# Shift rows in front of the sums, and query products in cycles of 18 score tiles

## The chip, the cores and the metric

The kernel runs on one core of a Trainium2 chip. The metric is the device time of one launch in microseconds (us), the median of several runs. Of the core's engines, TensorE (PE; its weight loads are listed apart as PEld) does the matrix products, ScalarE (ACT) the exponentials, VectorE (DVE) copies, reductions and splits, GpSimd (POOL) squares and some preparation, and SyncE (SP) issues the transfers.

## The reference

Two layers of attention and two of a token mixer, in turn, with the same weights both times. x is 2048 x 512, float32.

```python
x = x + A(layernorm(x)); x = x + B(layernorm(x))      # and both once more

def A(x):                                  # 32 heads of 16, one shared key and value head
    q = heads(x @ wq); k = x @ wk; v = x @ wv
    p = softmax(q k^T / 4)
    return concat(p v) @ wo

def B(x):                                  # over the tokens, F = 1792
    u = gelu(layernorm(x)^T @ w1 + b1)
    return (u @ w2 + b2)^T
```

## The kernel before

**Attention in score tiles.** The queries of a layer are 32 groups: 4 blocks of 512 queries, each with 8 groups of 4 heads. A group takes 32 score tiles, one for each of 16 key tiles and each of two pairs of heads, so a layer has 1024. A score tile is two matmuls into one of three double banks of PSUM (`scores`, L952), 51 rows deep: the queries and keys are split in a rounded part and a rest, and three rows more carry the shift. ScalarE takes exp into SBUF (L962). Every few tiles VectorE first copies the tile out of PSUM (L960) so that the bank comes free early, and ScalarE then works in SBUF; a "copied" tile below is such a one. Then come the sums (L968): two matmuls that multiply the exps by the values and a column of ones, each into its own strip of 32 columns of the group's bank. [...] Sums lag behind scores by two tiles at the end of a cycle. When a group's last sum is done, VectorE copies its bank out (L870), and divisions and the output product follow as side work.

**Cycles.** What order PE works in is written out in `Attention.run` by tuples. A number k > 0 means k tiles' scores, 13 a trio whose last tile is copied, -4 the sums of the four oldest tiles, 0 a piece of other work. The rest of an attention layer's query products are such pieces up to tile 256 or so, each of two halves of 6 matmuls (`in_halves`, L462 for the matmuls):

- WHOLE, 12 tiles: `(13, 0, 0, 13, -4, 13, -4, 13, -4)`, both halves behind the first trio.
- LONG, 16 tiles: `(2, 0, 13, -4, 13, -4, 13, 0, 13, -4, 12, -4)`, the halves apart.
- TINY, 4 tiles: `(2, 0, 2, -4)`, the piece being the shift rows of a block.
- PLAIN, 2 tiles, with no piece.

`Proj.later` (L688) lists the pieces in order; `run` takes the head of that list, turns WHOLE into LONG where there is slack, and takes PLAIN where a cycle would reach over a guard (a branch at tiles 64 and 256 of layer 0, 128 and 256 of layer 1, behind which the kernel picks the way by a bound of the scores). In the first drain behind a product's second half, `put_queries` rounds the queries (VectorE, L554 and L569), squares them (GpSimd, L565) and stores them to DRAM (SP, L574). From there `load_group` brings a group's queries (L831) and shift rows (L824) to one of two buffers.

**Shift rows.** For each block, `shifts` (L584 to L596) multiplies the squared queries by `sel`, a table that sums a head's 16 rows. Its four matmuls (L590), one for each 128 rows of queries, add into the same 32 rows of a PSUM bank, a row for each head. VectorE takes their minimum over the block (L594) and copies them (L595), and SP stores them (`put_shifts`, L757). The minima go by DRAM to one row (`store_lowest` L641, `load_lowest` L646), from which the guard's flag is worked out.

**The bank of a piece.** Pieces use the bank that the next group's sums will use (`spare`), so a piece must be read out before that group's first sums. Behind tile 256 pieces are the mixer's products, in other cycles.

Of the kernel before, what the change touches and what calls it, by code (L numbers as in the profile page):

```python
# [38 lines left out]
WHOLE = (13, 0, 0, 13, -4, 13, -4, 13, -4)  # L39
LONG = (2, 0, 13, -4, 13, -4, 13, 0, 13, -4, 12, -4)  # L40
# [11 lines left out]
TINY = (2, 0, 2, -4)  # L52
# [37 lines left out]
def kernel(  # L90
# [40 lines left out]
    sel = cp.tile([P, ND, H], BF16, tag="sel", name="sel")  # L131
# [3 lines left out]
    qmin = cp.tile([H, NB + 1], F32, tag="qmin", name="qmin")  # L135
# [5 lines left out]
    fd = dp.tile([3, H, NB], F32, tag="fd", name="fd")  # L141
# [18 lines left out]
    def constants():  # L160
# [19 lines left out]
        for m in range(ND):  # L180

            nc.gpsimd.affine_select(
                sel[:, m, :], sel[:, m, :], pattern=[[-DH, H]], compare_op=ALU.is_ge,
                fill=0.0, base=P * m, channel_multiplier=1,
            )
            nc.gpsimd.affine_select(
                sel[:, m, :], sel[:, m, :], pattern=[[DH, H]], compare_op=ALU.is_ge,
                fill=0.0, base=DH - 1 - P * m, channel_multiplier=-1,
            )
# [84 lines left out]
    class Proj:  # L274
# [11 lines left out]
        def open(self):  # L286
# [6 lines left out]
            self.c2 = k.tile([H, 2, QB], F32R, tag="c2", name=f"c2_{n}")  # L293
# [44 lines left out]
        def empty(self, eng=None):  # L338
            eng = eng or nc.vector
            if self.l == 0:  # L340
                nc.vector.memset(f32(self.wkv), 0.0)
            eng.memset(f32(self.c2), 0.0)
            self.ones = self.pool.tile([P, P], F32, tag="ones", name=f"ones{self.l}")
            eng.memset(self.ones, -SHIFT)
# [241 lines left out]
        def shifts(self, b, pc=None, parts=range(ND)):  # L586

            pc = (bank2(f"pc{self.l}_{b}")[:, 0, :] if pc is None else pc)[:H, :]
            for m in parts:
                nc.tensor.matmul(  # L590
                    pc, sel[:, m, :], self.sq.pop((b, m)), start=(m == parts[0]), stop=(m == parts[-1])
                )
            c = b + 1 if b or parts[0] else 0
            nc.vector.tensor_reduce(qmin[:, c : c + 1], pc, axis=AX.X, op=ALU.min)  # L594
            nc.vector.tensor_copy(self.c2[:, 0, :], pc)  # L595
            put_shifts(self.c2, NG * b + 2 * parts[0], NG * b + 2 * parts[-1] + 2, 8 * parts[0])  # L596
# [46 lines left out]
        def load_lowest(self, j, k):  # L643

            self.far = sm.tile([1, H, NB - 1], F32, tag="far", bufs=1, name=f"far{self.l}_{j}")
            nc.sync.dma_start(self.far[:, :, :k], fd[j : j + 1, :, :k])  # L646
# [40 lines left out]
        def later(self, att):  # L687

            n, work = self.l, []
# [7 lines left out]
            def rows(b, parts=range(ND)):  # L697
                put(TINY, [lambda i: self.shifts(b, bank(i, f"pc{n}_{b}"), parts)])

            def far(j, lo, hi):  # L700
                then(-1, lambda: self.lowest(j, lo, hi))
# [5 lines left out]
            if n == 0:  # L707
                project(0, range(2, ND))
                then(-1, lambda: (self.first.release(), att.weights()))
                rows(0, range(1, ND))  # L710
# [18 lines left out]
            for j in range(2 - n):  # L729
                k = j + (3 if n == 0 else 2)  # L730
                then(k, lambda j=j: att.split_weights(j))
            far(2, 2, NB + 1)
            return work
# [100 lines left out]
    class Attention:  # L834
        def __init__(self, layer):
# [5 lines left out]
            self.behind, self.lag, self.pieces = None, LAG, []  # L841
# [181 lines left out]
        def slack(self, later):  # L1023

            left = 2 * NKT * NG - self.scored - sum(self.size(t) for t, _, _ in later)
            return left - (48 if self.scored < 2 * NKT * 5 else 12)

        def run(self, mix, proj):
# [10 lines left out]
            while self.scored < total:  # L1039
                mix.chores(self)  # L1040
                ahead = min(t for t in guards if t > self.scored)
                known = ahead < guards[-2] or not later
# [3 lines left out]
                if turn is None:  # L1046
                    turn = PLAIN
                    self.lag = 2 * LAG if mix.normed and self.scored < total - 16 else LAG
                    if len(self.pend) == self.lag:
                        after, queued = None, bool(later) and not mix.projections  # L1050
                        if queued:
                            turn, parts, after = later[0]
                            if turn is WHOLE and self.to_boundary() >= 14 and self.slack(later) >= 4:
# [6 lines left out]
                    if queued and turn is LONG and left < self.size(LONG):  # L1060
# [7 lines left out]
                    if turn is WHOLE and self.to_boundary() == 2:  # L1068
                        turn = PLAIN
                parts = list(parts)  # L1070
                for k in turn:
                    if k > 0:
                        self.more(mix, k)
                    elif k == 0:
                        if queued and turn is TINY:
# [828 lines left out]
```

## Time and profile before

| | |
|---|---|
| time, median of 3 runs | 2494.57 us (2494.18 to 2497.32) |
| the profiled execution | 2495.04 us, span 2493.2, granted clock 0.998 |
| tiles 12 to 244, layer 0 | 232.60 us (57.67 to 290.27) |
| tiles 12 to 244, layer 1 | 227.13 us (1302.06 to 1529.19) |
| scores on PE, L952 | 684.8 us, sums L968 1000.4 us |
| exps on ACT, L962 | 1406.5 us from PSUM, 655.8 us from copied tiles |
| query products L462 | 81.0 us in 312 matmuls of the common form |
| shift rows: L590, L594, L595 | 8.3, 6.1 and 6.0 us |

Times in the table are busy times of groups but for the first four rows. A row of the timeline gives a start, a length, the engine, the line, what is written from what, and how many instructions it holds; in brackets stands how long the engine was idle before, and what ended that. A PE row's length runs to the end of its last matmul, which reaches into the next row; differences of starts are the better measure of what a row costs. A row of the waits gives a sum, a count and the longest.

### The profile page before, as it was taken

How to read it: one execution, taken by the hardware profiler on the slowest of the kernel's cores; microseconds unless marked ns; L12 is line 12 of the kernel's file. 1: busy time of each engine (PE TensorE's matmuls, PEld its weight loads, DVE VectorE, ACT ScalarE, POOL GpSimd, SP SyncE). 2: the span in 40 equal slices, each digit the busy share in tenths (PEclk: the TensorE clock that was granted, in tenths of full speed). 3: DMA queues.
4: the chain of work that ended last, by engine and by line, in shares of the span. 5: the costliest groups of instructions: out<-in, count | busy, mean ns of one | idle time of the engine just before them, and what ended most of it. 6: DMA issues, size and time to landing. Idle time of an engine off the chain costs nothing. (4 is left out here: it accounts for less than half of the span.)

```text
span 2493.2 us, 43495 instructions
## 1 busy us (share of the span) xinstructions
PE 2476.1 (99%) x16704; PEld 1253.2 (50%) x16704; DVE 1693.1 (68%) x2691; ACT 2148.4 (86%) x2430; POOL 160.6 (6%) x288
## 2 busy tenths in 40 slices
PE   9999999999999999999999999999999999999999
PEld 6444344444444444489964443444444444445898
DVE  6565566667766776579954664666677667765797
ACT  6999999999999999754459999999999999996643
POOL 5000000000000000140320000000000000002300
PEclk9999999999999999999999999999999999999999
DMA  3231201111111111153253211111111111111543
GB/s 126 75 98 44 66 27 39 34 39 31 39 32 41 31 40 31 33 152 89 60 184 118 59 48 49 31 39 31 40 31 40 32 41 31 40 31 44 143 119 94
DMA packets 168528, 147.80 MB, mean 59 GB/s; under 512 B 16723, under 2 KB 132977, under 8 KB 167537
## 3 DMA queue, kind: packets, MB, share of 16 engines
q1 hardware_dynamic: 168304, 144.85, 19.6%
q8 instruction: 137, 2.24, 0.4%
q14 instruction: 87, 0.70, 0.1%
HBM read 99.17 MB, written 28.84 MB: 51 GB/s over the span
## 5 line engine op out<-in xcount | busy, mean ns | idle before, releaser
L962 ACT ACTIVATE p<-sc 128x1024 f32<-128x1024 f32 x1444 | 1406.5, 1049 | 64.2 <-PE sc L952 63.1
L960 DVE COPY p<-sc 128x1024 f32<-128x1024 f32 x604 | 739.2, 1224 | 522.6 <-PE sc L952 437.8
L968 PE MATMUL acc<-p,vaug 128*32 128x512 f32 x8192 | 1000.4, 600 | 0.0
L952 PE MATMUL sc<-qs,kst 51*128 51x512 f32 x4096 | 684.8, 432 | 7.2 <-SPq L668 3.4
L962 ACT ACTIVATE p<-p 128x1024 f32<-128x1024 f32 x604 | 655.8, 1086 | 13.6 <-DVE p L960 8.8
L952 PEld LDWEIGHTS sc<-qs,kst 51*128 51x128 f32 x4096 | 338.3, 185 | 561.5 <-ACT p L962 387.8
L968 PEld LDWEIGHTS acc<-p,vaug 128*32 128x32 f32 x8192 | 218.9, 109 | 488.9 <-issue 473.6
L1247 PE MATMUL pu<-hb,w 128*128 128x512 f32 x792 | 209.7, 406 | 0.0
L1234 POOL TENSOR_TENSOR w<-w1r,w 128x256 fp32r<-128x256 f32 x86 | 68.5, 806 | 1583.3 <-ACT w L1232 1583.1
L1247 PEld LDWEIGHTS pu<-hb,w 128*128 128x128 f32 x792 | 140.9, 188 | 57.7 <-issue 31.8
L1476 ACT CAST w<-rA 128x896 fp32r<-128x896 f32 x88 | 82.8, 944 | 95.8 <-PE pyX L1598 46.1
L888 DVE RECIPROCAL o<-o 128x128 f32<-128x128 f32 x120 | 113.3, 944 | 8.9 <-DMA o<-ev 8.9
L1477 DVE TENSOR_TENSOR w<-rA,w 128x896 fp32r<-128x896 f32 x88 | 95.5, 1087 | 14.4 <-ACT w L1476 13.5
L929 PE MATMUL po<-wo,hl 128*128 128x512 f32 x360 | 100.7, 413 | 0.1
L1598 PE MATMUL pyY<-u,w 128*128 128x256 f32 (+1 forms) x392 | 88.7, 328 | 0.0
L870 DVE COPY ev<-acc 128x512 f32<-128x512 f32 x64 | 43.7, 683 | 62.8 <-PE acc L968 62.8
L462 PE MATMUL pq<-hT,wq 128*128 128x512 f32 x312 | 81.0, 403 | 0.0
L929 PEld LDWEIGHTS po<-wo,hl 128*128 128x128 f32 x360 | 62.6, 188 | 34.0 <-issue 16.0
L1247 PE MATMUL pu_l<-hb,w 128*128 128x512 f32 x336 | 77.1, 389 | 0.0
L1232 ACT CAST w<-w1r 128x256 fp32r<-128x256 f32 x86 | 34.1, 406 | 49.4 <-PE pu_l L1247 14.1
L1598 PEld LDWEIGHTS pyY<-u,w 128*128 128x128 f32 x392 | 68.4, 189 | 6.5
L1598 PE MATMUL pyX<-u,w 128*128 128x256 f32 (+1 forms) x420 | 70.9, 325 | 0.0
(232 smaller groups left out, 1795.4 us busy)
## 6 DMA issues: line engine op xcount, KB each, us to landing
w1r<-in_B_w_dram SPq DMA_DIRECT2D x224, 128.0 KB
rA<-in_B_w_dram SPq DMA_DIRECT2D x64, 448.0 KB
qs<-qd SPq DMA_DIRECT2D x384, 64.0 KB
qd<-q SPq DMA_DIRECT2D x64, 256.0 KB
o<-ev SPq DMA_DIRECT2D x128, 128.0 KB
x<-in_A_x_dram SPq DMA_DIRECT2D x16, 256.0 KB
hd<-hT SPq DMA_DIRECT2D x2, 2048.0 KB
out_dram<-x SPq DMA_DIRECT2D x10, 256.0 KB
```

What stands on the lines that cost most here:

```text
L462: yield nc.tensor.matmul(out, a, c, start=(k == 0), stop=(k == len(terms) - 1))
L888: nc.vector.reciprocal(o[:, 1, c], o[:, 1, c])
L929: nc.tensor.matmul(po, a, c, start=(k == 0), stop=(k == 3 * len(parts) - 1))
L952: nc.tensor.matmul(sc[:, j, :], kst[kt // 4][rows, kt % 4 * P : (kt % 4 + 1) * P], qs[i % NQ][rows, j0 // 2, :], start=True, stop=True,)
L960: nc.vector.tensor_copy(pt, sc)
L962: nc.scalar.activation(pt, sc, AF.Exp, scale=0.25)
L968: nc.tensor.matmul(self.acc[i][c : c + 32, :], vaug[:, kt].rearrange("p d k -> p (d k)"), pt[:, j, :], start=(kt == 0), stop=(kt == NKT - ...
L1234: eng.tensor_tensor(w[:, 1], raw, f32(w[:, 0]), op=ALU.subtract)
L1247: nc.tensor.matmul(pu, a, c, start=(start and k == 0), stop=(stop and k == 5))
L1476: nc.scalar.copy(out[:, 0], src)
L1477: nc.vector.tensor_tensor(out[:, 1], src, f32(out[:, 0]), op=ALU.subtract)
L1598: nc.tensor.matmul(out, a, c, start=start and k == i == 0 and len(terms) == 3, stop=(k == NFH - 1 and i == len(terms) - 1), skip_group_che ...
```

## The change

A new cycle BROAD of 18 tiles holds both halves behind its first trio, as WHOLE does, and then five trios more. `run` takes it for a query product with a slack of 6 tiles or more, in layer 0 only if no shift rows hang on the product; otherwise LONG or WHOLE as before. TINY is gone. The shift rows become a `tail` of the product in front of them, run in front of the sums of a later drain of the same cycle (the third behind the product), or of the PLAIN cycle that follows; until then no other piece is begun. The four matmuls of the rows now each write their own 32 rows of the bank, so that `sel` is one table instead of four, `qmin` and the copy cover 128 rows, and the rows of a block go out in four transfers of 8 rows instead of one of 32. The two calls of `split_weights` and the bound's load move by one entry with it.

```diff
+BROAD = (13, 0, 0, 13, -4, 13, -4, 13, -4, 13, -4, 13, -2)
-TINY = (2, 0, 2, -4)
...
-        def shifts(self, b, pc=None, parts=range(ND)):
-            pc = (bank2(f"pc{self.l}_{b}")[:, 0, :] if pc is None else pc)[:H, :]
+        def shifts(self, b, pc=None, parts=range(ND), new=0):
+            pc = bank2(f"pc{self.l}_{b}")[:, 0, :] if pc is None else pc
             for m in parts:
                 nc.tensor.matmul(
-                    pc, sel[:, m, :], self.sq.pop((b, m)), start=(m == parts[0]), stop=(m == parts[-1])
+                    pc[H * m : H * m + H, :], sel, self.sq.pop((b, m)), start=True, stop=True,
+                    skip_group_check=True,
                 )
...
-            nc.vector.tensor_reduce(qmin[:, c : c + 1], pc, axis=AX.X, op=ALU.min)
-            nc.vector.tensor_copy(self.c2[:, 0, :], pc)
-            put_shifts(self.c2, NG * b + 2 * parts[0], NG * b + 2 * parts[-1] + 2, 8 * parts[0])
+            nc.vector.tensor_reduce(qmin[rows, c : c + 1], pc[rows, :], axis=AX.X, op=ALU.min)
+            nc.vector.tensor_copy(self.c2[rows, 0, :], pc[rows, :])
+            for m in parts[new:]:
+                put_shifts(self.c2, NG * b + 2 * m, NG * b + 2 * m + 2, H * m)
...
-            def rows(b, parts=range(ND)):
-                put(TINY, [lambda i: self.shifts(b, bank(i, f"pc{n}_{b}"), parts)])
+            def rows(b, parts=range(ND), new=0):
+                tails[len(work) - 1] = [lambda i: self.shifts(b, bank(i, f"pc{n}_{b}"), parts, new)]
...
-                        after, queued = None, bool(later) and not mix.projections
-                        if queued:
-                            turn, parts, after = later[0]
-                            if turn is WHOLE and self.to_boundary() >= 14 and self.slack(later) >= 4:
+                        after, queued = None, bool(later) and not mix.projections and not self.tail
+                        if self.tail:
+                            turn, parts = PLAIN, []
+                        elif queued:
+                            turn, parts, after, tail = later[0]
+                            room = self.slack(later) if turn is WHOLE and (self.l or not tail) else 0
+                            if room >= 6:
+                                turn = BROAD
+                            elif room >= 4 and self.to_boundary() >= 14:
                                 turn = LONG
...
+                        elif self.tail and not parts and self.drains and self.to_boundary() >= -k > 0:
+                            spare = self.spare()
+                            for part in self.tail:
+                                part(spare)
+                            self.tail = None
...
+                        elif self.tail and not parts:
+                            self.drains = 1
                         self.drain(-k)
```

Between tiles 12 and 244, layer 0 had 12 WHOLE, 4 LONG, 4 TINY and 4 PLAIN cycles and now has 3 BROAD, 10 WHOLE, 3 LONG and 5 PLAIN; layer 1 had 11 LONG, 2 WHOLE, 4 TINY and 8 PLAIN and now has 9 BROAD, 1 WHOLE, 3 LONG and 5 PLAIN (two of the LONG in each, before and now, hold output projections).

**Order on TensorE, layer 1, the first cycle behind tile 12.** `sc_g_k_j` is the score tile of group g, key tile k and pair j, `acc` the sums, `pq` a query product. Before (LONG, its first half):

```order
L952 MATMUL sc_0_6_0_14099<-qs_93,kst_89 128x512 x2
L952 MATMUL sc_0_6_2_14104<-qs_93,kst_89 128x512 x2
L462 MATMUL pq_2_3_14109<-hT_2_13544,wq_13390 128x512 x6
L952 MATMUL sc_0_7_0_14116<-qs_93,kst_89 128x512 x2
L952 MATMUL sc_0_7_2_14121<-qs_93,kst_89 128x512 x2
L952 MATMUL sc_0_8_0_14126<-qs_93,kst_90 128x512 x2
L968 MATMUL acc_0_14036<-p_0_5_0_14084,vaug 32x512 x2
```

and now, the start and the end of BROAD:

```order
L953 MATMUL sc_0_6_0_14113<-qs_93,kst_89 128x512 x2
L953 MATMUL sc_0_6_2_14118<-qs_93,kst_89 128x512 x2
L953 MATMUL sc_0_7_0_14123<-qs_93,kst_89 128x512 x2
L459 MATMUL pq_2_3_14129<-hT_2_13557,wq_13402 128x512 x12
...
L969 MATMUL acc_0_14050<-p_0_12_0_14237,vaug 32x512 x2
L969 MATMUL acc_0_14050<-p_0_12_2_14242,vaug 32x512 x2
L953 MATMUL sc_0_13_2_14258<-qs_93,kst_91 128x512 x2
L953 MATMUL sc_0_14_0_14263<-qs_93,kst_91 128x512 x2
L953 MATMUL sc_0_14_2_14268<-qs_93,kst_91 128x512 x2
L969 MATMUL acc_0_14050<-p_0_13_0_14247,vaug 32x512 x2
L969 MATMUL acc_0_14050<-p_0_13_2_14261,vaug 32x512 x2
```

Both halves now stand together behind three tiles, and the cycle ends with a trio and two sums, the last of them of a tile whose scores stand three rows above it.

**Order on TensorE, layer 0, the shift rows of block 1.** `pc` is the rows' bank, `sq` the squared queries. Before:

```order
L952 MATMUL sc_3_3_0_2062<-qs_94,kst_88 128x512 x2
L952 MATMUL sc_3_3_2_2067<-qs_94,kst_88 128x512 x2
L590 LDWEIGHTS sel
L590 MATMUL pc_1_2076<-sq_1_0_1403,sel 32x512
...
L590 MATMUL pc_1_2076<-sq_1_3_1982,sel 32x512
L952 MATMUL sc_3_4_0_2084<-qs_94,kst_89 128x512 x2
L952 MATMUL sc_3_4_2_2089<-qs_94,kst_89 128x512 x2
L968 MATMUL acc_3_2050<-p_3_2_0_2042,vaug 32x512 x2
```

and now:

```order
L953 MATMUL sc_3_6_2_2114<-qs_94,kst_89 128x512 x2
L953 MATMUL sc_3_7_0_2119<-qs_94,kst_89 128x512 x2
L953 MATMUL sc_3_7_2_2124<-qs_94,kst_89 128x512 x2
L587 LDWEIGHTS sel
L587 MATMUL pc_1_2130<-sq_1_0_1322,sel 32x512
...
L587 MATMUL pc_1_2130<-sq_1_3_2074,sel 32x512
L969 MATMUL acc_3_2021<-p_3_5_0_2090,vaug 32x512 x2
L969 MATMUL acc_3_2021<-p_3_5_2_2095,vaug 32x512 x2
```

The four row products stood between scores and now stand between scores and sums.

**Order on SP where layer 1 begins.** `cd` holds the shift rows and `qd` the queries in DRAM, `fd` and `far` the minima. Before:

```order
L757 DMA cd<-c_1_13392 16x1024
L641 DMA fd<-qmin 32x1
L646 DMA far_0_13649<-fd 1x32x1
L831 DMA qs_93<-qd 16x2x512 x6
L824 DMA qs_93<-cd 2x2x512 x2
```

and now:

```order
L758 DMA cd<-c_1_13404 8x1024 x2
L641 DMA fd<-qmin 128x1
L647 DMA far_0_13663<-fd 1x32x1
L832 DMA qs_93<-qd 16x2x512 x6
L825 DMA qs_93<-cd 2x2x512 x2
```

One transfer of rows has become two; the loads behind it are the same.

More of the change, by code (lines that the diff above doesn't have):

```diff
@@ L179, in constants @@
         nc.gpsimd.memset(sel, -SHIFT)
[L180 to L189, printed above, removed]
+        nc.gpsimd.affine_select(
+            sel, sel, pattern=[[-DH, H]], compare_op=ALU.is_ge, fill=0.0, base=0, channel_multiplier=1
+        )
+        nc.gpsimd.affine_select(
+            sel, sel, pattern=[[DH, H]], compare_op=ALU.is_ge, fill=0.0, base=DH - 1, channel_multiplier=-1
+        )
         return pk
@@ L342, in empty @@
             eng.memset(f32(self.c2), 0.0)
+            eng.memset(qmin, 0.0)
             self.ones = self.pool.tile([P, P], F32, tag="ones", name=f"ones{self.l}")
@@ L687, in later @@
         def later(self, att):
-            n, work = self.l, []
+            n, work, tails = self.l, [], {}
             def put(turn, parts):
@@ L709, in later @@
                 then(-1, lambda: (self.first.release(), att.weights()))
-                rows(0, range(1, ND))
+                rows(0, range(ND), 1)
                 far(1, 1, 2)
@@ L1023, in slack @@
         def slack(self, later):
-            left = 2 * NKT * NG - self.scored - sum(self.size(t) for t, _, _ in later)
+            left = 2 * NKT * NG - self.scored - sum(self.size(entry[0]) for entry in later)
             return left - (48 if self.scored < 2 * NKT * 5 else 12)
@@ L1041, in run @@
                 ahead = min(t for t in guards if t > self.scored)
-                known = ahead < guards[-2] or not later
+                known = ahead < guards[-2] or not (later or self.tail)
                 if ahead < total and self.scored >= ahead - 16 and flagged < ahead and known:
@@ L1059, in run @@
                     left = min(t - self.scored for t in guards if t > self.scored)
-                    if queued and turn is LONG and left < self.size(LONG):
+                    if queued and turn in (LONG, BROAD) and left < self.size(turn):
                         turn = WHOLE
@@ L1067, in run @@
                         turn = PLAIN
-                    if turn is WHOLE and self.to_boundary() == 2:
+                    if turn in (WHOLE, BROAD) and self.to_boundary() == 2:
                         turn = PLAIN
@@ L1074, in run @@
                     elif k == 0:
-                        if queued and turn is TINY:
-                            mix.step(2.0, self)
                         parts.pop(0)(self.spare())
@@ L1105, in run @@
                             mix.step(2.0, self)
-                assert self.scored < guards[-2] or not later
+                assert self.scored < guards[-2] or not (later or self.tail)
                 if self.scored in guards[:-1] and self.scored > guarded:
@@ L1665, in pc @@
         def pc():
-            nc.tensor.matmul(halves("pc", 0)[:H, :], sel[:, 0, :], proj.sq.pop((0, 0)), start=True, stop=True)
+            nc.tensor.matmul(halves("pc", 0)[:H, :], sel, proj.sq[0, 0], start=True, stop=True)
         def c2():
-            nc.scalar.copy(proj.c2[:, 0, :], halves("pc", 0)[:H, :])
+            nc.scalar.copy(proj.c2[:H, 0, :], halves("pc", 0)[:H, :])
         def qmin_():
-            nc.vector.tensor_reduce(qmin[:, :1], halves("pc", 0)[:H, :], axis=AX.X, op=ALU.min)
+            nc.vector.tensor_reduce(qmin[:H, :1], halves("pc", 0)[:H, :], axis=AX.X, op=ALU.min)
         def pq():
```

31 lines of the change are left out of this document (17 added, 14 removed).

## The prediction, made before the changed kernel was run

> **What bounds the kernel now.** I read the page's busy shares first, then the waits, then the busy time by stretch for tiles 12 to 244 of both attention layers, where the change works, and for two steady stretches behind tile 256, then the timeline of one cycle of each kind. The shares and two waits:
>
> ```profile
> span 2493.2 us, 43495 instructions
> PE 2476.1 (99%) x16704; PEld 1253.2 (50%) x16704; DVE 1693.1 (68%) x2691; ACT 2148.4 (86%) x2430; POOL 160.6 (6%) x288
> PEld sc L952 <- ACT p L962: 387.8, 512, 1.7
> PEld acc L968 <- ACT p L962: 10.4, 34, 0.8
> ```
>
> TensorE is busy 99% of the span. Its weight loads for scores wait for exps often (512 times, for the bank), those for sums seldom. The stretches (length; then PE, PEld, DVE, ACT, POOL busy; clock; DMA share; GB/s), tiles 12 to 244 of layer 0 and of layer 1, then the steady part of each:
>
> ```profile
> 57.67:290.27 232.60, 231.78 (x1604) 98.78 (x1600) 136.76 (x176) 217.85 (x233) 14.59 (x14) 1.00 0.24 69
> 1302.06:1529.19 227.13, 226.49 (x1566) 92.05 (x1563) 128.13 (x175) 217.95 (x233) 11.46 (x11) 1.00 0.25 73
> 315.11:1038.00 722.89, 722.37 (x5068) 300.73 (x5068) 495.38 (x771) 702.24 (x753) 0.00 (x0) 1.00 0.11 34
> 1553.95:2276.00 722.05, 721.54 (x5066) 300.38 (x5064) 496.14 (x772) 701.72 (x753) 0.00 (x0) 1.00 0.11 34
> ```
>
> PE covers 99.6% and 99.7% of the first two; 232 tiles take 1.003 us each in layer 0 and 0.979 in layer 1. ACT is busy 94% and 96% there, so little lies between the two limits: whatever PE saves beyond about 5% turns into a wait for an exp. Behind tile 256 the instruction order of both kernels is the same, so the sum concerns 460 us.
>
> **A cycle of today.** One WHOLE cycle (12 tiles, product whole):
>
> ```profile
> 164.40 0.96 PE L952 MATMUL sc<-qs,kst 51*128 51x512 f32 x6
> 165.29 3.02 PE L462 MATMUL pq<-hT,wq 128*128 128x512 f32 x12
> 168.25 0.97 PE L952 MATMUL sc<-qs,kst 51*128 51x512 f32 x6
> 168.84 1.94 ACT L962 ACTIVATE p<-sc 128x1024 f32<-128x1024 f32 x2 [0.88 <-PE sc L952]
> 169.14 1.92 PE L968 MATMUL acc<-p,vaug 128*32 128x512 f32 x16
> 171.00 0.96 PE L952 MATMUL sc<-qs,kst 51*128 51x512 f32 x6
> 171.62 1.94 ACT L962 ACTIVATE p<-sc 128x1024 f32<-128x1024 f32 x2
> 171.89 1.92 PE L968 MATMUL acc<-p,vaug 128*32 128x512 f32 x16
> 172.34 0.13 PEld L968 LDWEIGHTS acc<-p,vaug 128*32 128x32 f32 x4 [0.30 <-issue]
> 173.43 1.08 ACT L962 ACTIVATE p<-p 128x1024 f32<-128x1024 f32 x1
> 173.74 0.96 PE L952 MATMUL sc<-qs,kst 51*128 51x512 f32 x6
> 174.37 1.96 ACT L962 ACTIVATE p<-sc 128x1024 f32<-128x1024 f32 x2
> 174.63 1.92 PE L968 MATMUL acc<-p,vaug 128*32 128x512 f32 x16
> 175.47 0.18 PEld L968 LDWEIGHTS acc<-p,vaug 128*32 128x32 f32 x6 [0.26 <-ACT p L962]
> 176.49 0.96 PE L952 MATMUL sc<-qs,kst 51*128 51x512 f32 x6
> ```
>
> A trio of scores takes 0.89 (171.00 to 171.89), four sums 1.85 (171.89 to 173.74), the product 2.96 (165.29 to 168.25). A WHOLE cycle is 4 x 0.89 + 3 x 1.85 + 2.96 = 12.07 of PE back to back, 12.09 by its rows (164.40 to 176.49). During the product ACT runs dry (0.88 idle at 168.84) and then PE bounds the rest. The row at 175.47 is the near miss: the load for D1's sum (the cycle's fourth trio, first tile) waits 0.26 for the exp begun at 174.37 and may go 1.10 after that start. It costs nothing here, as the matmuls of the earlier sums still run.
>
> The other kinds, LONG (16 tiles, halves apart), TINY (shift rows) and PLAIN:
>
> ```profile
> 1360.35 0.73 PE L952 MATMUL sc<-qs,kst 51*128 51x512 f32 x4
> 1375.82 0.96 PE L952 MATMUL sc<-qs,kst 51*128 51x512 f32 x6
> ```
>
> ```profile
> 200.66 0.73 PE L952 MATMUL sc<-qs,kst 51*128 51x512 f32 x4
> 201.33 1.04 PE L590 MATMUL pc<-sq,sel 128*32 128x512 bf16 x4
> 202.29 0.73 PE L952 MATMUL sc<-qs,kst 51*128 51x512 f32 x4
> 204.81 1.06 PE L952 MATMUL sc<-qs,kst 51*128 51x512 f32 x6
> 292.18 0.73 PE L952 MATMUL sc<-qs,kst 51*128 51x512 f32 x4
> 294.02 0.73 PE L952 MATMUL sc<-qs,kst 51*128 51x512 f32 x4
> ```
>
> LONG 15.47 (1360.35 to 1375.82), TINY 4.15 (200.66 to 204.81), of it 0.96 for four row products one after another (201.33 to 202.29), PLAIN 1.84. These prices reproduce the stretches: 12 WHOLE, 4 LONG, 4 TINY, 4 PLAIN make 230.9 of 232.60 in layer 0, 11 LONG, 2 WHOLE, 4 TINY, 8 PLAIN make 225.7 of 227.13 in layer 1; the 1.5 left is at the guards and stays.
>
> **The change, term by term.** By the order of the cycles, layer 0 goes to 3 BROAD, 10 WHOLE, 3 LONG, 5 PLAIN, layer 1 to 9 BROAD, 1 WHOLE, 3 LONG, 5 PLAIN, 232 tiles each; every TINY goes, and eight sets of row products stand in front of sums.
>
> *BROAD.* On PE alone it is 6 x 0.89 + 4 x 1.85 + 2.96 + 0.93 (two sums) = 16.63. But its exps must keep up. I walk it with the rows above, time 0 at the first score behind the product: trio B's scores 0 to 0.89, its sums to 2.74, C to 5.48, D to 8.22. Exps start 0.60 after their scores (168.84 less 168.25) and about 0.9 apart. E's scores start 8.22, E1's exp 8.84, E2's 9.74. E's drain takes D2, D3, E1, E2; E2's slot is at 10.46 (9.11 and three times 0.45, the spacing of the loads at 171.89 and 172.34), but E2 is there at 9.74 + 1.10 = 10.84: PE waits 0.38. With E2's sum at 0.46, F's scores start 11.30, F1's exp 11.90, ready 13.00, where its slot was 12.64: another 0.36. So BROAD is 16.63 + 0.74 = 17.37, say 17.4: 0.967 a tile, exactly as LONG, and better than WHOLE (1.008). In WHOLE the sums lag the exps by enough; two more trios without a product use that up.
>
> *Cycles without row products.* Layer 0: 3 x 17.4 + 1.84 - 2 x 12.09 - 15.47 - 4 x 4.15 = -2.2. Layer 1: 9 x 17.4 - 8 x 15.47 - 12.09 - 4 x 4.15 - 3 x 1.84 = -1.4.
>
> *Row products in front of sums*, r for each of eight. They are four matmuls as before, but each writes its own strip of 32 columns. Not under 0.24, since four together can't be shorter than one alone (0.96/4). Not over today's 0.96. The nearest row is that of the sums, which also use 32-column strips of one bank: their loads come four at a time, 0.13 for the four, ahead of matmuls still running (172.34), and sixteen matmuls take 1.85, 0.116 each. I take 0.24, and keep 0.96 for the range.
>
> The Trainium skill speaks against that: "TensorE: Matmul & The Clock Gate", Part 3 (What overlaps and what doesn't), says that a weight load overlaps running matmuls only when its row group differs, and here all four share all 128 rows. By that r would be about 0.96. Its table in the same part has three column tiles 2.38 times as fast as in a row, which agrees with the row at 172.34.
>
> *VectorE.* The reduction and the copy of the rows now cover 128 rows instead of 32 and stand between two copied tiles:
>
> ```profile
> 172.07 1.23 DVE L960 COPY p<-sc 128x1024 f32<-128x1024 f32 x1 [0.20 <-PE sc L952]
> 202.69 0.67 DVE L594 TENSOR_REDUCE qmin<-pc 32x1 f32<-32x512 f32 x1
> 203.29 0.67 DVE L595 CAST c<-pc 32x512 fp32r<-32x512 f32 x1
> ```
>
> As they run along 512 columns either way, I leave 0.67 each; 128 partitions were free for the 1024-column copy too. Copy, reduction and cast are 2.57 in a trio's 2.74, so they fit; with a division step of 0.8 behind them the next copied tile is up to 0.6 late, which its sum, a drain later, does not see. If it did, 8 x 0.6 = 4.8 would be the price.
>
> *SP.* A block's rows are stored by four transfers instead of one. That shows only where layer 1 begins, with two blocks' rows waited for:
>
> ```profile
> 1278.47 0.36 SPq L757 DMA_DIRECT2D cd<-c  x1
> 1281.31 2.86 SPq L831 DMA_DIRECT2D qs<-qd  x6
> 1284.20 1.41 SPq L824 DMA_DIRECT2D qs<-cd  x2
> 1286.46 0.47 PE L952 MATMUL sc<-qs,kst 51*128 51x512 f32 x1 [0.22 <-DMA qs<-cd]
> ```
>
> The first score waits for the last of these loads, so one more store ahead of them is +0.4. In layer 0 the store of a query product now stands ahead of the load for group 2:
>
> ```profile
> 171.90 1.25 SPq L574 DMA_DIRECT2D qd<-q  x2
> 109.32 0.93 PE L952 MATMUL sc<-qs,kst 51*128 51x512 f32 x4 [0.63 <-PEq L668]
> ```
>
> The second row is that group's first score today (tile 64). The product begins near tile 45, some 19 tiles or 18 us earlier; its store goes out 6.6 after its start (165.29 to 171.90), so at about 97.5, and the load, 4.3 in the queue and about 1 to land by the rows of the entry, is there near 104: an estimate that leaves 5 to spare, so nothing. On GpSimd six table instructions go and a memset grows, both on the way in beside the first loads; I put them at nothing, and at the page's 160.6 us of POOL work in the whole run they are well below what I can tell.
>
> *Sum.* -2.2 - 1.4 + 0.4 + 8r: -1.3 at r = 0.24, +4.5 at 0.96. The profiled execution is 2495.04 us, its span and 1.84 around it, 0.47 above the median of the runs; so 2495.04 - 1.3, less 0.47: **2493.3**.
>
> **Rivals.**
>
> *Faster: BROAD at PE's own 16.63.* If E2 and F1 are not waited for, as exps that start earlier would allow, another 12 x 0.74 = 8.9 come off: 2484.4. For it: waits of sums on exps are 10.4 us in the whole run, 34 times. Against it: 175.47 shows the wait already there at the end of a WHOLE cycle, and ACT has only some 5% in hand. Half of it, 2489, is about the edge of what can be told. A chance of 0.15.
>
> *Slower: the row products go one after another in front of sums.* Then sums and all that follows shift by 0.96 each time: +4.5, 2499.1. The kernel is slower than before from r = 0.40 on, and by over 0.2% from 1.02, so by a little more than today's price. For it: they do so today (201.33). Against it: today all four add into the same 32 rows, and the sums in strips don't. By the Trainium skill's rule on weight loads, named above, this would be the case. A chance of 0.17, of it 0.1 beyond 0.2%, with the late copied tile above as what would carry it there.
>
> *The forecast itself:* TINY's 0.96 goes and 0.24 comes, the pairs of halves gain per tile over WHOLE in layer 0 and nothing over LONG in layer 1. A chance of 0.68.
>
> 0.2% is 5.0 us, about what a measurement of this kernel can tell from no change: faster 0.15, slower 0.10, and the same 0.75 (the forecast and the rest of the second rival). The range reaches from half of the first rival to the second with a little room: 2489 to 2500.
>
> **What would show it.** Tiles 12 to 244 should take about 231.4 us in layer 0 (2.2 less, 4 x 0.24 more) and 226.7 in layer 1. A BROAD cycle should read 17.4 from first trio to next first trio, with two waits of sums on exps near its end, so some 24 more entries and 9 us more in that group of waits; 16.6 would mean the faster rival. The row products should start within 0.3 of the sums behind them; 0.9 or more would mean the slower one. The layer-1 entry should have its first score 0.4 later against the far load. I am wrong if BROAD stays at PE's sum, if a copied tile after the row products holds up a bank, or if anything behind tile 256 changes length.

## The result, and the profile after

The changed kernel takes 2516.36 us (median; 2515.31 to 2518.0) beside 2494.56 for the kernel before: 1.0088 times as long, 95% interval 1.0078 to 1.0098. The forecast was 2493.3 with a range of 2489 to 2500, so it was wrong, and on the side to which it had given 0.10. The page and the waits of the kernel after, the lines that answer to those of before:

```profile
span 2515.9 us, 43533 instructions
PE 2492.1 (99%) x16705; PEld 1255.8 (50%) x16705; DVE 1711.6 (68%) x2707; ACT 2147.6 (85%) x2430; POOL 159.7 (6%) x284
PEld sc L953 <- ACT p L963: 386.7, 514, 1.7
PEld acc L969 <- ACT p L963: 34.3, 65, 0.9
```

TensorE is as busy as before, 99% of a longer span. What has changed is the last row: sums wait for exps 34.3 us in 65 places, where it was 10.4 in 34. (The profile holds each matmul of the sums twice, 8192 records for 2048 tiles, so in the rows below x4 of L969 is the sums of one tile.)

Where the time went is read by stretch (columns as in the prediction: length, then PE, PEld, DVE, ACT and POOL busy, clock, DMA share, GB/s). Kernel after, tiles 12 to 244 of layer 0 and layer 1, then tiles 244 to 270 of each, which hold the guard at tile 256:

```profile
60.40:295.02 234.62, 233.76 (x1605) 98.76 (x1601) 141.19 (x178) 218.07 (x233) 14.56 (x14) 1.00 0.24 68
1310.32:1545.76 235.44, 234.51 (x1562) 92.85 (x1558) 137.60 (x173) 218.00 (x233) 11.45 (x11) 1.00 0.21 64
295.02:323.92 28.90, 26.24 (x160) 7.83 (x157) 11.54 (x32) 24.04 (x27) 0.00 (x0) 0.88 0.22 62
1545.76:1576.58 30.82, 26.30 (x165) 7.95 (x161) 11.52 (x30) 24.08 (x27) 0.00 (x0) 0.89 0.28 73
```

Kernel before, the two stretches at the guard:

```profile
290.27:315.11 24.84, 24.06 (x160) 7.71 (x157) 9.38 (x25) 24.02 (x27) 0.00 (x0) 1.00 0.23 68
1529.19:1553.95 24.76, 23.98 (x158) 7.71 (x157) 5.75 (x14) 23.94 (x27) 0.00 (x0) 1.00 0.09 29
```

Against before, layer 0's tiles 12 to 244 take 2.0 more (232.60), layer 1's 8.3 more (227.13), the guards 4.1 and 6.1 more. That is 20.5 of the 22.6 by which the profiled spans differ. Tile 12 of layer 0 starts 2.7 later (60.40 against 57.67), and the rest is 0.6 shorter. No run here shows these 2.7 to be an effect of the change (see the run with 32 rows at the first guard). So there are two places to explain: the cycles, and a guard whose instruction order the prediction had found the same. The clock column of the last rows (0.88 and 0.89 instead of 1.00) belongs to the guard.

**The end of BROAD.** Kernel after, layer 1, a BROAD without row products; the cycle starts at 1384.31 and the next at 1402.70, 18.39 later:

```profile
1384.31 0.96 PE L953 MATMUL sc<-qs,kst 51*128 51x512 f32 x6
1396.39 0.96 PE L953 MATMUL sc<-qs,kst 51*128 51x512 f32 x6
1397.03 1.97 ACT L963 ACTIVATE p<-sc 128x1024 f32<-128x1024 f32 x2
1397.29 2.82 PE L969 MATMUL acc<-p,vaug 128*32 128x512 f32 x16
1398.14 0.15 PEld L969 LDWEIGHTS acc<-p,vaug 128*32 128x32 f32 x4 [0.70 <-ACT p L963]
1399.05 0.14 PEld L969 LDWEIGHTS acc<-p,vaug 128*32 128x32 f32 x4 [0.77 <-ACT p L963]
1400.04 0.98 PE L953 MATMUL sc<-qs,kst 51*128 51x512 f32 x6
1400.94 1.83 PE L969 MATMUL acc<-p,vaug 128*32 128x512 f32 x8
1401.72 0.14 PEld L969 LDWEIGHTS acc<-p,vaug 128*32 128x32 f32 x4 [0.63 <-ACT p L963]
1402.70 0.96 PE L953 MATMUL sc<-qs,kst 51*128 51x512 f32 x6
```

The waits that cost time stand just where the walk of the prediction had put them, at E2 (1399.05) and F1 (1401.72). (E1's load at 1398.14 waits too, but goes 0.85 after the pair in front of it, about when that pair is through.) But four sums take 2.75 there (1397.29 to 1400.04) instead of 1.85, and two take 1.76 (1400.94 to 1402.70) instead of 0.93. From the load for E2 to the next scores it is 0.99, where the prediction had 0.46 for a tile.

**The guard.** Kernel after, layer 0, SP's and TensorE's rows from the last row products to the first tiles behind the guard:

```profile
294.30 0.68 DVE L593 TENSOR_REDUCE qmin<-pc 128x1 f32<-128x512 f32 x1
295.60 1.34 SPq L758 DMA_DIRECT2D cd<-c  x4
299.21 0.71 SPq L647 DMA_DIRECT2D far<-fd  x1
299.97 4.73 SPq L1236 DMA_DIRECT2D w1r<-in_B_w_dram  x7
304.76 1.24 PE L969 MATMUL acc<-p,vaug 128*32 128x512 f32 x8
308.60 2.68 SPq L832 DMA_DIRECT2D qs<-qd  x6
308.66 1.42 PE L953 MATMUL sc<-qs,kst 51*128 51x512 f32 x4 [2.66 <-SPq L669]
311.88 1.22 PE L953 MATMUL sc<-qs,kst 51*128 51x512 f32 x4
314.89 0.75 PE L953 MATMUL sc<-qs,kst 51*128 51x512 f32 x4
```

SP stores the rows, reads the bound back, issues seven loads for the mixer that starts here, ends at 304.70, and passes the guard (L669) only 3.9 later. Of these 3.9, its records give 0.6 to loading the flag and branching (304.75 to 305.34) and 0.65 to the semaphores in front of the next load (307.95 to 308.60); in the 2.6 between them SP has no record at all. At the guards at other tiles of this run that gap is 0.14 to 0.48; what fills it here stays open. TensorE is done with its sums at 306.00 and waits for SP until 308.66. Then the next two pairs of tiles take 3.22 and 3.01 (308.66 to 314.89), where a pair took 1.83 before the change. The clock says why:

```profile
304.70:308.60 3.90, 1.30 (x10) 0.29 (x8) 0.00 (x0) 2.02 (x3) 0.00 (x0) 0.94 0.28 79
308.60:315.00 6.40, 6.34 (x26) 1.75 (x26) 0.69 (x1) 3.88 (x4) 0.00 (x0) 0.50 0.31 99
```

TensorE is granted half its clock for 6.83 us by the clock records of the trace (308.13 to 314.96). Before the change the last rows came 4 tiles earlier here (16 in layer 1), and SP had ended its loads at 296.06, 5 us before TensorE came to the guard (301.42, as 0.78 before the third row):

```profile
287.51 0.34 SPq L757 DMA_DIRECT2D cd<-c  x1
290.24 5.82 SPq L1224 DMA_DIRECT2D w1r<-in_B_w_dram  x7
302.20 0.91 PE L952 MATMUL sc<-qs,kst 51*128 51x512 f32 x4 [0.78 <-DMA qs<-qd]
304.03 0.73 PE L952 MATMUL sc<-qs,kst 51*128 51x512 f32 x4
```

### The profile page after: what moved, and what is told of

It is laid out like the page before. It is cut to its first block, busy times and chain, and to the rows that moved or that the text cites. A ratio compares the mean times of both kernels' runs of the same rounds, so it can differ in the third digit from the quotient of the medians.

```text
span 2515.9 us, 43533 instructions
## 1 busy us (share of the span) xinstructions
PE 2492.1 (99%) x16705; PEld 1255.8 (50%) x16705; DVE 1711.6 (68%) x2707; ACT 2147.6 (85%) x2430; POOL 159.7 (6%) x284
## 5 line engine op out<-in xcount | busy, mean ns | idle before, releaser
L963 ACT ACTIVATE p<-sc 128x1024 f32<-128x1024 f32 x1428 | 1390.9, 1047 | 88.2 <-PE sc L953 86.9
L961 DVE COPY p<-sc 128x1024 f32<-128x1024 f32 x620 | 758.9, 1224 | 537.5 <-PE sc L953 441.9
L969 PE MATMUL acc<-p,vaug 128*32 128x512 f32 x8192 | 1024.4, 602 | 0.4 <-DVE q L566 0.4
L963 ACT ACTIVATE p<-p 128x1024 f32<-128x1024 f32 x620 | 673.3, 1086 | 12.6 <-DVE p L961 8.2
L969 PEld LDWEIGHTS acc<-p,vaug 128*32 128x32 f32 x8192 | 220.9, 109 | 505.4 <-issue 465.4
```

The costliest lines, as they stand in the source:

```text
L961: nc.vector.tensor_copy(pt, sc)
L963: nc.scalar.activation(pt, sc, AF.Exp, scale=0.25)
L969: nc.tensor.matmul(self.acc[i][c : c + 32, :], vaug[:, kt].rearrange("p d k -> p (d k)"), pt[:, j, :], start=(kt == 0), stop=(kt == NKT - ...
```

## The experiments

Two theories stand against each other in most runs: that the loss is the end of BROAD plus SP's lateness at the guard, or that something else (the rows in front of the sums, ScalarE's rate, the bound's own chain) is behind it. Stretch lengths below are read as above, in each run's own trace.

**BROAD with its last two drains swapped.**

```diff
-BROAD = (13, 0, 0, 13, -4, 13, -4, 13, -4, 13, -4, 13, -2)
+BROAD = (13, 0, 0, 13, -4, 13, -4, 13, -4, 13, -2, 13, -4)
```

> The changed kernel with the end of BROAD written (..., 13, -2, 13, -4) instead of (..., 13, -4, 13, -2); nothing else. In the changed kernel a BROAD cycle took 18.39 us where no shift rows stand in it, 1.0 more than forecast. Theory: the two last drains wait for exps that have only just begun, and sums of a single tile that start after such a wait can't run beside another tile's, so a wait of 0.4 costs 0.9, twice in a cycle. With the drains swapped no drain reaches a tile of the trio in front of it except the last, as in WHOLE, so BROAD should take 17.3 to 17.5, and the 12 of them give back about 12 us: 2504 to 2505. Rival: BROAD is slow because ScalarE falls behind by the whole product or because copied tiles hold banks; then the order of the drains does not matter, 18.3 or more a cycle and 2515 to 2517.

Measured: 2507.39 us, 1.0053 of before [1.0036, 1.0070], 9.0 less than the changed kernel, if not the 2504 to 2505 expected. Tiles 12 to 244 take 232.13 and 228.21 (2.5 and 7.2 less), a BROAD without rows 17.58. The end of such a cycle in this run:

```profile
1389.16 0.96 PE L953 MATMUL sc<-qs,kst 51*128 51x512 f32 x6
1390.05 1.07 PE L969 MATMUL acc<-p,vaug 128*32 128x512 f32 x8
1391.05 0.51 PE L953 MATMUL sc<-qs,kst 51*128 51x512 f32 x2
1391.82 0.73 PE L953 MATMUL sc<-qs,kst 51*128 51x512 f32 x4 [0.27 <-ACT p L963]
1392.48 2.25 PE L969 MATMUL acc<-p,vaug 128*32 128x512 f32 x16
1394.66 0.73 PE L953 MATMUL sc<-qs,kst 51*128 51x512 f32 x3
```

Two sums take 1.00 now (1390.05 to 1391.05, where the next scores begin), the trio behind them waits for banks that exps have yet to free, and the last four sums still take 2.18. So 0.81 of the 1.0 came back per cycle. The guards took 29.38 and 32.29, no less than in the changed kernel (28.90 and 30.82): they are a loss of their own.

**A tile's sums alone: drains of 5 and 3 in the kernel before.**

```diff
-WHOLE = (13, 0, 0, 13, -4, 13, -4, 13, -4)
+WHOLE = (13, 0, 0, 13, -5, 13, -3, 13, -4)
```

> The kernel before with WHOLE's drains of 4, 4, 4 tiles made 5, 3, 4; same cycles, same work, nothing of the change. It measures what a tile's sums cost that stand alone. Theory (sums go two tiles at a time, four strips side by side, 0.88 a pair, and a lone tile costs as much as a pair): 5 and 3 tiles take 3 + 2 pairs' time instead of 4, so a WHOLE cycle goes from 12.09 to 12.9 to 13.0, and with 14 such cycles the time is 2504 to 2507. Rival (0.46 a tile, as the prediction had it): 12.1 and 2494 to 2496.

Measured: 2508.79 us, 1.0051 [1.0036, 1.0066], above the 2504 to 2507 expected, though the cycles came as expected: tiles 12 to 244 take 243.63 and 228.86, 11.0 and 1.7 more than before. Most WHOLE cycles go from 12.09 to 12.92 or 12.97. Rows of one that takes 12.92:

```profile
175.71 2.77 PE L968 MATMUL acc<-p,vaug 128*32 128x512 f32 x20
178.40 0.96 PE L952 MATMUL sc<-qs,kst 51*128 51x512 f32 x6
179.30 1.91 PE L968 MATMUL acc<-p,vaug 128*32 128x512 f32 x12
181.14 0.97 PE L952 MATMUL sc<-qs,kst 51*128 51x512 f32 x6
```

Three tiles' sums (12 records) take 1.84, as long as four; five take 2.69. With nothing of the change in it, and no wait of sums for an exp in these rows, this shows the price that the prediction lacked: sums go in pairs of tiles, as a tile fills only two of the four strips of columns, and a tile without a partner costs the whole pair. In BROAD's end each wait separates a pair.

**The mixer's first splits and their loads behind the guard.** The splits free the buffers for which three of the seven loads wait.

```diff
-            if 2 * NKT * 8 <= scored and self.done == 0 and not self.w1:
+            if 2 * NKT * 8 < scored and self.done == 0 and not self.w1:
```

> The changed kernel with the mixer's first three weight splits, and so the three w1r loads that wait for their buffers, behind the guard at tile 256 instead of in front of it. In the changed kernel the first score behind that guard waits 2.66 (layer 0) and 4.52 us (layer 1) for SP, and TensorE's granted clock is 0.50 for some 6 us after that, about 4.1 and 6.1 us in all. Theory A: SP reaches the guard late because seven loads stand in its queue behind the late bound; with four instead of seven it comes about 2 earlier in layer 0, where the wait and the half clock should vanish (-4), and in layer 1 the wait shrinks to about 2 (-2 to -5): 2507 to 2510. Theory B: the loads do not matter, the flag itself is late (SP goes on 6.3 us after the flag is written in both layers); then both waits stay and the time is 2515 to 2517.

Measured: 2508.01 us, 1.0055 [1.0038, 1.0072], 8.3 less than the changed kernel; in the traces 2.5 of that is an earlier tile 12 (57.91), which is not the edit's. Tiles 244 to 270 take 24.73 in layer 0 (before the change 24.84) and 27.05 in layer 1; behind the guard of layer 0 the clock stays at 1.00. Layer 0 later gives back 2.0: from tile 270 to the layer's last tile it takes 724.31, where the changed kernel takes 722.30 and only the other runs with these loads behind the guard take over 723. Theory A holds in layer 0, and in layer 1 the wait shrank from 4.52 to 1.80 and the clock still dipped (0.94 in the mean).

**The change without BROAD.**

```diff
-                            if room >= 6:
+                            if room >= 2000:
                                 turn = BROAD
```

> The changed kernel without BROAD: query products go to LONG where the slack is 4 or more, else WHOLE; the shift rows stay in front of the sums. Tiles 12 to 244 then hold 10 WHOLE, 6 LONG, 8 PLAIN in layer 0 and 3 WHOLE, 10 LONG, 18 PLAIN in layer 1, whose last rows come some 16 tiles earlier than in the changed kernel, while layer 0's come at the same tile. Theory (BROAD's end and the late bound are the loss, rows in front of sums cost about 0.24): layer 0's stretch 231, layer 1's 226.4, layer 1's wait at tile 256 gone, layer 0's still there: 2497 to 2499. Rival (the rows in front of sums are the loss, by a wait behind them): both stretches stay above 232 and the time is over 2505.

Measured: 2498.21 us, 1.0011 [1.0002, 1.0021]; tiles 12 to 244 230.45 and 226.46, the guards 28.88 and 24.95. So the rows in front of sums, with the cycles that TINY's end leaves room for, made both stretches shorter than before, by 2.1 and 0.7. A WHOLE that holds row products takes 12.28 instead of 12.09. Layer 1, whose last product ends 16 tiles earlier here, has no wait at its guard; layer 0, whose rows come at the same tile as in the change, has it in full. What keeps the time above that of before is layer 0's guard (4.0) and, in this trace, an entry that is 1.3 longer.

**The rows in their old form, in front of the sums.** The kernel before with the shift rows as tails, no BROAD, and the four products still adding into 32 rows (so one store for a block). Of the edit, the line that makes the rows a tail:

```diff
-                put(TINY, [lambda i: self.shifts(b, bank(i, f"pc{n}_{b}"), parts)])
+                tails[len(work) - 1] = [lambda i: self.shifts(b, bank(i, f"pc{n}_{b}"), parts)]
```

> The kernel before with the shift rows in front of the sums and nothing else of the change: no BROAD, and the four row products still add into the same 32 rows, with one transfer for a block. Its cycles are those of the run without BROAD (2498.2 us), so it differs from it by the form of the rows alone. Theory: four products into the same rows run one after another, 0.96 instead of the 0.22 they take side by side in the changed kernel, and nothing hides it: each of eight sets costs 0.7 more, tiles 12 to 244 take 230.45 + 2.9 and 226.46 + 2.9, about 5.5 in all, against which one transfer instead of four brings the last bound in layer 0 about 1 earlier: 2502 to 2504. Rival: the products hide behind the exps that the sums wait for, in either form; then both stretches stay within 0.8 of the run without BROAD, 2497 to 2499.

Measured: 2495.35 us, 1.0006 [0.9996, 1.0015], against 2502 to 2504 expected: a miss, and a useful one. In layer 0 the form does cost what was thought: 232.82 against 230.45, and a WHOLE with rows takes 12.91 instead of 12.28, so 0.82 against 0.19 above a WHOLE without. In layer 1 the difference is only 1.3 for four sets, all of which fall into PLAIN cycles there. Such a PLAIN takes 2.49 instead of 1.84 for four row products. But behind the first two sets stands a product's cycle, and in the first of them the run without BROAD waits 0.45 for a bank that an exp has yet to free, while this run does not; from the start of the PLAIN to the end of that cycle it is 14.72 against 14.57. The last two sets, with no product behind them, cost 0.57 and 0.56 more. And layer 0's guard took 24.92 instead of 28.88, though its rows come at the same tile. With one store of 0.35 instead of four in 1.34, SP ended its loads 9.37 after the reduction's start instead of 10.37, and TensorE came to the guard 12.34 after it instead of 11.70, as its rows took longer. So the wait was 0.93 instead of 2.66, and the clock did not fall. Differences of 1.0 and 0.64 decided 4.0 us at the guard.

**Rows 6 tiles earlier in layer 0.** The change without BROAD, with 32 rows at the first guard (below), and

```diff
-            return left - (48 if self.scored < 2 * NKT * 5 else 12)
+            return left - (48 if self.scored < 2 * NKT * 5 else 12) - (12 if self.l == 0 else 0)
```

> The changed kernel without BROAD, with the first guard's minima as 32 rows, and in layer 0 with 12 tiles more of slack asked for before a product goes to LONG, so that the last product and its rows come 6 tiles earlier (WHOLE from tile 226 instead of 232). Without the two other edits (run without BROAD) layer 0 took 28.88 us from tile 244 to 270, 4.0 more than before the change, layer 1, whose rows came 16 tiles early, 24.95. Theory (a late bound is the whole loss at the guard): layer 0's 244 to 270 goes to 24.8, tiles 12 to 244 to 230.5 to 231.2: 2493 to 2495, level with the kernel before or up to 2 faster. Rival (the guard's wait comes from the four transfers and the 128 rows, whenever they come): 28 or more stays there and the time is 2497 or more.

Measured: 2492.36 us, 0.9994 [0.9985, 1.0003]: level with the kernel before, the lowest median of all runs. The guard takes 24.75, so its loss comes from lateness and not from the form of the rows as such. The stretch in front of it is 232.01, longer than the 230.5 to 231.2 expected and 1.56 more than without BROAD: 0.3 for a LONG that became a WHOLE and two PLAIN (15.77 against 15.47), 0.8 in the last WHOLE with rows (13.10 instead of 12.28) and 0.45 in the product that now stands right behind the guard at tile 64 (12.54 instead of 12.09).

**The bound in front of the rows on SP.** Minima stored and read back ahead of the four stores of the rows, tried on the change without BROAD (with 32 rows at the first guard) and on the change itself. `shifts` returns its four stores as a function, which the tail calls last:

```diff
-                tails[len(work) - 1].append(lambda i: self.lowest(j, lo, hi))
+                tails[len(work) - 1].insert(1, lambda i: self.lowest(j, lo, hi))
```

> The run without BROAD (2498.2 us) with two edits: the first guard's minima as 32 rows, and in each tail that holds a bound the minima's store and read-back stand on SP in front of the four stores of the rows instead of behind them. The cycles stay as they were, so layer 0's last rows come as late as in the changed kernel. There the four stores take 1.34 us and the minima's store starts 2.0 after the reduction's end. Theory (the guard's loss is a cliff: a chain 1 to 2 us late costs a wait of 2.66 at which TensorE's clock halves): the minima leave about 1.5 to 2 earlier, the wait falls under 1, the half clock vanishes, layer 0 from tile 244 to 270 goes from 28.9 to about 25.0, and nothing else moves: 2493 to 2495. Rival (the wait is set by the loads in SP's queue and the branch, not by when the minima leave): 28 or more stays, 2496 to 2498.

> The changed kernel with that one edit: minima stored and read back in front of the four stores of the rows; BROAD as in the change. Theory: layer 0's 244 to 270 goes from 28.9 to about 25, and in layer 1, where the wait was 4.52, it shrinks to about 2.6, near the 2.66 at which the clock still fell, so 30.8 goes to 27 to 29; the BROAD cycles keep their 18.39: 2509 to 2511. Rival as above: both stay, 2515 to 2517.

Measured: 2494.51 us, 1.0004 [0.9995, 1.0013], and 2515.06 us, 1.0086 [1.0071, 1.0102]. The first time lies in the range expected (2493 to 2495), but not for the reason given, and the second misses (2509 to 2511): the waits at layer 0's guard stayed at 2.64 and 2.62. In layer 1 of the second the wait fell from 4.52 to 3.60, and tiles 244 to 270 still took 31.38. The bound was early, but the four stores then stood ahead of the mixer's loads, the splits waited 1.74 for the first load, and SP came as late as ever. So it is the end of SP's loads that counts, as the rival had it. The runs show one more thing. With nearly the same wait, tiles 244 to 270 of layer 0 took 28.88 (run without BROAD, wait 2.66), 27.77 (wait 2.64) and 26.53 (wait 2.62), with 6.83, 3.41 and 0 us of half clock by the records. Against the 24.84 of before, a wait of this size costs 1.7 by itself, and the clock up to 2.35 more. The stretch in which it did not fall, in rows of the change with the bound first:

```profile
304.80:307.40 2.60, 0.00 (x1) 0.01 (x1) 0.00 (x0) 0.73 (x1) 0.00 (x0) 1.00 0.07 16
307.40:313.00 5.60, 5.58 (x36) 1.84 (x36) 0.69 (x1) 4.78 (x6) 0.00 (x0) 1.00 0.27 83
```

**Splits where they were, their three loads behind the guard.** The change without BROAD, with 32 rows at the first guard, and

```diff
                 for j in range(3):
                     self.split1(j)
+            if 2 * NKT * 8 < scored and self.done == 0 and max(self.raw1) == 3:
+                for j in range(3):
                     self.load1(j + 4)
```

> The run without BROAD (2498.2 us) with the first guard's minima as 32 rows, and the mixer's three weight splits where they were, in front of the guard at tile 256, while the three loads that wait for the buffers which the splits free go out behind it. The run with splits and loads behind the guard had lost the guard's wait in layer 0 but took 1.7 us more later, as its splits came late. Theory (SP comes late to the guard through the end of its loads): layer 0's 244 to 270 goes from 28.88 to 24.7 to 25.0 and the rest stays: 2492 to 2494, some 1 to 2 us faster than the kernel before, about what the stretches 230.45 and 226.46 against 232.59 and 227.13 would give with the entry. Rival (what helped there was the splits' absence on VectorE, not the loads on SP): 28 or more stays, 2496 to 2498.

Measured: 2493.72 us, 0.9994 [0.9985, 1.0003]. Layer 0's guard takes 24.67 with the splits back in front of it, so the three loads on SP were what made it late. Tiles 12 to 244 are 230.44 and 226.39, as short as without BROAD. Part of the gain is lost again behind tile 270 (723.46 against 722.93 before), and the entry of its profiled execution was a long one (59.78), so it is level with the kernel before and not shown to beat it.

**32 rows at the first guard.** The first guard's minima stored and read back as before. The store's line, the one that reads back being changed to match:

```diff
-            nc.sync.dma_start(fd[j, :, : hi - lo], qmin[:, lo:hi])
+            nc.sync.dma_start(fd[j, : H if self.l + j == 0 else P, : hi - lo], qmin[: H if self.l + j == 0 else P, lo:hi])
```

> The changed kernel with the minima of the first guard of layer 0 stored and read back as 32 rows, as before, instead of 128. In the changed kernel tile 12 of layer 0 starts 2.7 us later: 0.6 are there from the way in, the first scores come 0.45 later against the loads' issue, and TensorE's clock is 0.50 for about 6.5 us instead of 3.3 behind the first guard. Theory: the 128 small pieces delay the queries' bound rows behind them on the queues, and the longer half clock follows from that; 2 to 2.5 us come back: 2514. Rival: the half clock's length goes by when its windows happen to fall, not by this store; then less than 0.6 comes back, 2516.

Measured: 2513.0 us, 1.0080 [1.0064, 1.0097], lower than either theory gave, but an interval that overlaps that of the changed kernel. Tile 12 started at 56.68. But with the change's own entry it started at 60.40, 58.00, 57.91, 58.96 and 59.26 in five kernels, with this edit at 56.68, 58.27, 58.21, 57.72 and 59.78, and with the old entry at 57.67, 60.09 and 59.89. These overlap throughout, so the 2.7 us seen in the one profile lie within the scatter of this stretch. The clock records sort them, as the rival had it: half clock between 46 and 56 us lasts 0 in the trace with 56.68, 3.41 in the seven with 57.67 to 58.96 (the kernel before among them), and 6.83 in the five with 59.26 to 60.40 (the changed kernel among them). Each group but the first, which is one trace, holds kernels of all three entries. What is left for the 128 rows is too small to tell.

**Three edits together.** Swapped drains, splits and loads behind the guard, 32 rows.

> The changed kernel with three of the edits tried alone before: BROAD ending (..., 13, -2, 13, -4), the mixer's first splits and their loads behind the guard at tile 256, and the first guard's minima as 32 rows. Alone the first two took 9.0 and 8.3 us off the changed kernel's 2516.4; the third took 3.4 off with a wide interval, since layer 0's entry scatters from 56.7 to 60.4 us from one profiled execution to the next. Theory: they lie in different stretches and add up: 2516.4 - 9.0 - 8.3 is 2499.1, less up to 2 for the entry: 2497 to 2499. Rival: they share the loss (a shorter BROAD only makes the late bound later against the guard), then 2502 or more.

Measured: 2498.52 us, 1.0015 [1.0006, 1.0025], within what adding them up gave (2497 to 2499). Stretches 232.13 and 228.26, guards 24.67 and 27.03: each edit on the cycles or the guard acts in its own stretch. BROAD, even with this end, leaves layer 1 1.1 longer than before.

## Why the prediction was wrong, point by point

**BROAD at 17.4: wrong, the term of the sum that was mis-sized.** The mechanism was right, the two waits and their places too. The step that failed is "With E2's sum at 0.46": it took a quarter of four sums as the price of one. The same reading gave each tile a slot of its own, "three times 0.45, the spacing of the loads". In that trace the sixteen records of the drain at 171.89 start in four groups of four (171.89, 172.34, 172.77, 173.20), and a group holds records of two tiles: 0.88 is the step of a pair, and no tile has a step of 0.45. The runs showed 0.98 and 0.99 for a tile that starts after its partner (the rows at 1401.72 and 1399.05) and 0.83 to 0.88 more for a WHOLE whose drains leave two tiles alone (the odd drains). The two waits of 0.38 and 0.36 became 0.90 and 0.83 of lost time, BROAD 18.39 instead of 17.37, and over 12 cycles that is about 12 us, of which the two stretches got 9.7 back when two drains were swapped. The walk counted what an engine waits and not what it can no longer do side by side.

**"Behind tile 256 the instruction order of both kernels is the same, so the sum concerns 460 us": wrong.** The order is the same, but the time at which SP comes to the guard is not. The prediction looked for SP at the entry of layer 1 and at the load for group 2, and not at the place where the rows were moved past: the last set went from tile 240 to 244 in layer 0 and from 230 to 246 in layer 1, its stores from 0.35 to 1.34, and behind them on SP stood the bound, seven loads and the guard. This term, put at nothing, was 4.1 and 6.1 us: it was gone in layer 1 with earlier rows (24.95 without BROAD), in layer 0 with earlier rows (24.75) and with the loads put behind the guard (24.73 and 24.67). A cost that starts as a wait of 2.66 was made larger by the clock.

The Trainium skill states in "TensorE: Matmul & The Clock Gate", Part 1 (What's actually happening), that the clock falls to half after an idle window of about 3.4 us, and that the windows run freely and do not start anew with a kernel. The traces agree with the half (0.50) and with the window's length (half clock lasts 3.41, 6.83 or 10.24 us behind these guards), and a free phase would explain why waits of 2.62 and 2.66 had different outcomes; they differ in that waits of 1.75 to 2.66 were enough here.

**Row products at r = 0.24: right.** The change's four products of a set start together and the sums follow 0.22 later (layer 1, kernel after):

```profile
1546.43 0.40 PE L587 MATMUL pc<-sq,sel 128*32 128x512 bf16 x4
1546.65 1.03 PE L969 MATMUL acc<-p,vaug 128*32 128x512 f32 x8
```

WHOLE with rows is 0.19 longer than without; in the old form, where their starts in the kernel before are 0.22 apart (201.33 to 201.98), it is 0.82. The rule of the Trainium skill that spoke against it ("TensorE: Matmul & The Clock Gate", Part 3, What overlaps and what doesn't) doesn't hold for these four strips of columns: four in 0.22, where it would give about 0.96 by the prediction's estimate.

**The sum without BROAD.** Rows in front and TINY gone were forecast as a gain, and without BROAD, in another mix of cycles, the stretches are 2.1 and 0.7 shorter than before. That part was right in sign; layer 0's late guard (4.0) took it back.

**VectorE, layer 1's entry.** Reduction and copy over 128 rows take 0.68 each, as forecast from 0.67. The first score of layer 1 comes 8.62 after the first store of its rows (1286.58 to 1295.20) instead of 7.99, so +0.6 where +0.4 was forecast; from that store to tile 12 it is 23.74 against 23.59.

**Signs and rivals.** The prediction named 24 more waits of sums on exps and 9 us more; they were 31 and 23.9, as E1 waits too. Copied tiles held up banks no more than before: scores' loads wait 18.6 us for VectorE's copies in the whole run, where it was 21.1. That something behind tile 256 would change length was a sign of being wrong, and it came. Neither rival came true. The faster one needed BROAD at 16.63; even with its drains swapped it takes 17.58, as its scores wait for banks that exps have yet to free. The slower one named the row products, which cost 0.19. The slower case that came was neither of them.

## What to carry to other kernels

When small matmuls run side by side in strips of the array, price them by the group that fills it: a wait that splits a group costs a whole group's time, not its share. When a step is moved later, follow each queue on which it issues to the next point where all engines meet, and compare the arrival there with the engine that has no time to lose. A late queue can be free up to a point and then cost more than it is late: at the guard of tile 256 no wait of 0.78 to 0.93 was followed by half clock in these traces, and 11 of the 12 waits of 1.75 to 4.52 were. And before a difference of a few microseconds between two profiles is put down to an edit, look whether their clock records differ.

## What was not expected of the hardware

Whenever its loads ended late, SP passed the guard at tile 256 3.8 to 4.2 us after their end (304.70 to 308.60 in the change, 297.81 to 301.69 with the bound first), though in the change the flag had been written 6 us before; in both of these 2.6 of it is the gap behind its branch, and layer 0 of the kernel before has such a gap too (2.78), where SP is early enough for it not to matter. Waits of 2.62, 2.64 and 2.66 us of TensorE at the same place were followed by 0, 3.41 and 6.83 us of half clock; in layer 1 a wait of 3.60 was followed by 10.24 and one of 4.52 by 6.83. And three kernels that share an entry of the same instructions reached tile 12 up to 2.4 us apart in their profiled executions (57.67 to 60.09 with the old entry), which is more than several edits of this study move: the first had 3.41 us of half clock on the way, the other two 6.83.
